# Channel attention over a 384 x 384 x 384 image: the untaken rewrite of the packed rows in two pieces instead of fourteen parts

## The chip, the cores and the metric

The kernel runs on one core of one Trainium2 chip. The metric is device time in microseconds (us). A kernel is timed in several runs, and one more execution is taken with the hardware profiler: it gives the profile page and the trace. All times inside that execution count from the start of its span, which goes from the first to the last instruction of the program.

The engines are PE (matrix multiplies), DVE (vector), ACT (scalar), POOL, and SP, which here does nothing but issue loads and wait. A name with a q (SPq, ACTq) means the engine's sequencer: transfers that it issues, branches, and instructions that only wait for or change a semaphore.

## The reference

`x` has 147,456 pixels of 384 channels in bf16. Over all pixels, each channel's mean and maximum go through a small two-layer network; the sum of both results goes through a sigmoid; and every pixel is multiplied by the 384 scales:

```python
xf = x.reshape(B, H * W, C)
gap = jnp.mean(xf, 1)
gmp = jnp.amax(xf, 1)
h_a = gap @ w1          # then the part below zero is set to zero
h_m = gmp @ w1          # likewise
scale = _sigmoid(h_a @ w2 + h_m @ w2)
return x * scale[:, None, None, :]
```

So `x` has to be read once for the scales, and then all of it has to be multiplied and written: 113 MB out, and 113 MB in at the first reading.

## The kernel before

**Rows.** The kernel lays the image out as 1,152 rows for each of the 128 partitions; a row is 384 channels of bf16, so one row over all partitions is 96 KB. `rows` is one large area of on-chip memory: five held rows, and `body` with 280 rows.

**First phase.** All rows are loaded on SP's queue (L373). PE adds them up for the mean, DVE takes the maximum into `acc` (L342). Rows that find no room are read again later. To keep more of them on the chip, 224 rows (`packed_block`, seven groups of 32) are packed: a group is four parts of eight rows, and after packing it takes up three (`homes`): two of them take the low bytes of the other two in place of their own high bytes, and the third holds the high bytes of all four in a shorter form (`pack`, L318). This shorter form holds only if the values lie in a certain range. ACT tests that on the way (`test`, L308), `judge` (L336) sums the findings, and L555 turns the sum into a flag.

**Second phase.** Once the scales are known (L433), a hand-written order takes turns: DVE multiplies a block (`multiply`, L436), ACT issues its store (`store`, L491, L492), and SP issues the next load of rows that were not kept (`read`, L518, L531) as soon as the place is free. Between them the packed groups are unpacked (`unpack`, L464), multiplied and stored (`finish`, L497). The last stores are those at L583, of ten rows kept in PSUM and of the late rows, which leave from `acc`.

**What follows the last store.** The flag is read into a register on SP, ACT and DVE (L556). `tc.If(bad != 0)` at L584 holds a rewrite: if the test failed, the packed rows are read once more, multiplied and stored over what was written. Each engine that takes part has a compare-and-branch there. If the flag is zero, it jumps over the rewrite.

**Semaphores, as the tile layer gives them out.** Each transfer adds 16 to one of eight semaphores (DMAHW0 to DMAHW7), taken in turn; DVE's instructions count up another. Whoever needs a transfer waits for its semaphore's count. Code behind the `If` has to find the same counts whichever way was taken. So the layer writes a second branch for the case "test passed": for each semaphore that the rewrite would raise, one instruction that waits until the main part's count is reached and then adds what the rewrite would have added. For the transfers' semaphores, SP has these; for DVE's count, DVE has one. The profile shows them under L584. Behind that stands the end of the program (L616, where the kernel's context is closed): SP waits for the final count of every semaphore, in seven instructions with two semaphores each, and then all engines meet at a barrier.

The instructions stand in the order of the code on each engine (`manual_schedule`, L199).

Of the kernel before, what the change touches and what calls it, by code (L numbers as in the profile page):

```python
# [9 lines left out]
ALU = mybir.AluOpType  # L10
# [22 lines left out]
PACKED = 7  # L33
# [6 lines left out]
FIRST_AT = (0, 104, 40, 64, 200, 176, 152)  # L40
FOURTH_AT = (24, 96, 32, 88, 128, 136, 144)
# [39 lines left out]
FIRST_PLACE = ((0, 8, (8, 8)), (0, 0, (8,)))  # L81
SECOND_PLACE = ((1, 0, (8, 9)), (2, 0, (10,)))
OTHER_PLACES = ((1, 17, (14,)), (2, 10, (24,)))
TEST_SCALE = 0.031187
SUM_TAIL = 4
MM_ROWS = 4
# [3 lines left out]
def kernel(  # L90
# [7 lines left out]
    nc = tc.nc  # L98
    P = nc.NUM_PARTITIONS
    B_, H, W_, C = x.shape  # L100
# [4 lines left out]
    GP = 4 * G  # L105
# [3 lines left out]
    xr = x.rearrange("b h w c -> (b h w) c")  # L109
    orr = out.rearrange("b h w c -> (b h w) c")  # L110

    def rows_of(ap, block):
        first, n = block
        return ap[first * P:(first + n) * P, :].rearrange("(p n) c -> p n c", n=n)
# [7 lines left out]
    def take(n):  # L122
        nonlocal at
        at += n
        return at - n, n
# [3 lines left out]
    packed_block = take(GP * PACKED)  # L129
# [26 lines left out]
    scale_bc = consts.tile([P, C], BF16)  # L156
# [9 lines left out]
    rows = nc.alloc_sbuf_tensor_at("rows", [P, HELD_ROWS + BODY_ROWS, C], BF16, offset=RING_BYTES).ap()  # L166
    held, body = rows[:, 0:HELD_ROWS, :], rows[:, HELD_ROWS:HELD_ROWS + BODY_ROWS, :]
    slots = [body[:, lo:lo + n, :] for lo, n in SLOTS]
    spare = body[:, SPARE, :]
    homes = [body[:, lo:lo + 3 * G, :] for lo in HOME_AT]  # L170
# [36 lines left out]
    nc.vector.memset(bank_a, 0.0)  # L207
    nc.vector.memset(test_bias, 4.5 * TEST_SCALE)
    nc.vector.memset(minus4, -4.0)
# [25 lines left out]
    for i in range(PACKED):  # L235
        if i in TOGETHER:
            lo = min(HOME_AT[i], D_AT[i % 2])
# [59 lines left out]
    def test_one(rows, k):  # L297
# [3 lines left out]
        if len(rows.shape) == 3:  # L301
            out_ = out_.rearrange("p (r n) -> p r n", r=rows.shape[1])
        nc.scalar.activation(out=out_, in_=rows, func=ACT.Square, bias=test_bias, scale=TEST_SCALE)  # L303
        nc.scalar.activation(  # L304
# [57 lines left out]
    for st in steps:  # L362
# [8 lines left out]
        _, block, rows, lo, hi = st  # L371
# [10 lines left out]
        j = max(0, min(m, A - done))  # L382
# [5 lines left out]
        while j < m:  # L388
            c, e = halves[turn % len(halves)]
# [33 lines left out]
    for q0, part_ps in tp_ps:  # L423
        n = part_ps.shape[1]
# [11 lines left out]
    def multiply(dst, src):  # L436
        n = dst.shape[1]
        nc.vector.tensor_tensor(  # L438
            out=dst, in0=src, in1=scale_bc.unsqueeze(1).to_broadcast([P, n, C]), op=ALU.mult
        )  # L440
# [16 lines left out]
    homes_d = [d_places[i % 2] for i in range(4)]  # L457
# [33 lines left out]
    def store(buf, block, lo):  # L491
        nc.scalar.dma_start(out=rows_of(orr, block)[:, lo:lo + buf.shape[1], :], in_=buf)  # L492
# [25 lines left out]
    def read(last_turn, blocks_gone):  # L518

        if not again:  # L520
            return False
        k = len(PLACES) - len(again)
        lo, n = PLACES[k]
        if lo + n > RING + 3 * G * blocks_gone or max(turn_of_row[lo:lo + n]) > last_turn:
            return False
        turn_of_row[lo:lo + n] = [k] * n
        buf, b = body[:, lo:lo + n, :], again.pop(0)
        assert b[1] == n
        j = 0
        for m in FIRST_READ if k == 0 else (n,):  # L530
            nc.sync.dma_start(out=buf[:, j:j + m, :], in_=rows_of(xr, b)[:, j:j + m, :])  # L531
            j += m
        assert j == n
        order.append((b, buf))
        return True

    def put_slot(i, lo, pieces):
        put(stay[i], slots[i][:, lo:, :], pieces, lo)
# [11 lines left out]
    read(-1, 0)  # L550
    for pieces in OTHER_PLACES:
        put_slot(*pieces)
# [7 lines left out]
    j = PLACES[-1][0] + PLACES[-1][1]  # L560
    assert j + for_psum <= PLACES[-5][0] + PLACES[-5][1]
    leaving = [(body[:, j:j + for_psum, :], first_block), (acc[:, 0:LATE_ROWS, :], late_block)]
    for turn in range(turns):
        b, buf = order.pop(0)
# [17 lines left out]
    for to, block in leaving:  # L582
        store(to, block, 0)  # L583
    with tc.If(bad != 0):  # L584
        for i in range(PACKED):
            for buf, lo in ((homes[i], FIRST_AT[i]), (homes_d[i], FOURTH_AT[i])):
                n = buf.shape[1]
                nc.sync.dma_start(out=buf, in_=rows_of(xr, packed_block)[:, lo:lo + n, :])
                multiply(buf, buf)
                store(buf, packed_block, lo)  # L590
    in_order.close()

# [28 lines left out]
```

## Time and profile before

| what | value |
|---|---|
| median of 3 runs | 725.27 us (725.21 to 725.94) |
| the profiled execution | 724.86 us, its span 723.07 us |
| busy: DVE, ACT, PE | 563.9, 349.8, 183.8 us |
| read and written | 192.14 and 113.25 MB, 422 GB/s over the span |
| shares of the queues of loads and of stores | 62.4% and 36.7% of the transfer engines' span |
| last store: issue, and time to landing | 682.98 us, 38.2 us |

How to read it: the share of a queue is the time that its packets took, against 16 transfer engines over the whole span. "Time to landing" counts from the issue of a transfer to the last raise of its semaphore. In the view of one line, the three numbers are the shortest, median and longest duration in ns, then the starts of the first and the last in us. In the view of waits, the numbers are the sum in us, how many waits, and the longest. Semaphore instructions and branches count as busy for no engine, so they stand in none of the shares of busy time.

### The profile page before, as it was taken

The numbers are of one execution on the slowest core, as the hardware profiler recorded it, in microseconds if no ns is written. First come the engines' busy times: TensorE is split into PE (matmuls) and PEld (weight loads), VectorE is DVE, ScalarE is ACT, GpSimd is POOL, SyncE is SP. The second block draws the span as 40 slices with busy tenths as digits, with TensorE's granted clock in tenths as the row PEclk, the third lists the DMA queues.
The fourth block names the chain that finished last, engine by engine and source line by source line (L and its number), as shares of the span: only waits on it lengthen the run. The fifth ranks groups of instructions, "written<-read, shape, count | busy, mean of one in ns | idle before, by whom it ended". The sixth has DMA issues, their size and how long they took to land.

```text
span 723.1 us, 3872 instructions
## 1 busy us (share of the span) xinstructions
PE 183.8 (25%) x1354; PEld 73.1 (10%) x1354; DVE 563.9 (78%) x441; ACT 349.8 (48%) x251; POOL 0.7 (0%) x6
## 2 busy tenths in 40 slices
PE   5577475966777560000000000000000000001000
PEld 1222122322222140000000000000000000001000
DVE  5698999999999998797966454798888889496200
ACT  6999999997999200057230032806244451300000
POOL 0000000000000000000000000000000000000000
PEclk9888878896978555555555555555555555555555
DMA  9999999999999979999999999999999999999997
GB/s 381 431 441 436 420 435 429 432 426 433 430 427 425 424 314 385 396 433 429 432 432 429 436 426 432 424 435 433 430 435 436 430 432 430 435 435 431 441 426 341
DMA packets 21123, 305.63 MB, mean 423 GB/s; under 512 B 2704, under 2 KB 2928, under 8 KB 8176
## 3 DMA queue, kind: packets, MB, share of 16 engines
q1 hardware_dynamic: 13760, 192.14, 62.4%
q10 hardware_dynamic: 7344, 113.25, 36.7%
q8 instruction: 10, 0.16, 0.1%
q14 instruction: 9, 0.07, 0.0%
HBM read 192.14 MB, written 113.25 MB: 422 GB/s over the span
## 4 chain that ended last, share of the span: by engine, by line
DMA 63%; DVE 28%; issue 3%; SPq 0%; DVEq 0%
DMA rows<-in_x_dram 44%; DVE acc L342 19%; DMA out_dram<-rows 18%; DVE rows L438 8%; DMA acc<-in_x_dram 1%; DVE rows L470 1%; DVE acc L438 0%; SPq L373 0%; DVE acc L475 0%; DVE acc L470 0%; SPq L531 0%; DVEq L438 0%; DVEq L342 0%
## 5 line engine op out<-in xcount | busy, mean ns | idle before, releaser
L438 DVE TENSOR_TENSOR rows<-rows,scale_bc 128x9216 bf16<-128x9216 bf16 (+9 forms) x56 | 230.9, 4166 | 93.7 <-DMA rows<-in_x_dram 92.7
L342 DVE TENSOR_TENSOR acc<-acc,rows 128x2304 bf16<-128x2304 bf16 (+4 forms) x234 | 245.2, 1126 | 12.7 <-DMA rows<-in_x_dram 12.5
L489 ACT COPY rows<-rows 128x1536 uint8<-128x1536 uint8 x28 | 41.3, 1476 | 206.4 <-DVE rows L438 205.7
L276 PE MATMUL bank_a<-rows,small 128*1 128x512 bf16 (+3 forms) x888 | 94.8, 473 | 82.0 <-DMA rows<-in_x_dram 82.0
L348 PE MATMUL words_ps<-ident_bf,acc 128*128 128x128 bf16 x24 | 2.7, 313 | 378.4 <-DVE acc L576 378.4
L303 ACT ACTIVATE rows<-rows 128x3072 uint8<-128x3072 int8 (+1 forms) x35 | 81.9, 2341 | 10.5 <-DMA rows<-in_x_dram 9.8
L304 ACT ACTIVATE rows<-rows 128x3072 uint8<-128x3072 uint8 (+1 forms) x35 | 82.0, 2344 | 1.1
L489 ACT COPY rows<-acc 128x1536 uint8<-128x1536 uint8 x42 | 60.5, 1473 | 18.2 <-DVE acc L475 17.7
L276 PEld LDWEIGHTS <-small 128*1 128x1 bf16 x888 | 30.4, 95 | 142.9 <-issue 122.0
L348 PEld LDWEIGHTS <-acc 128*128 128x128 bf16 x24 | 2.5, 148 | 378.6 <-DVE acc L576 378.6
L330 ACT COPY rows<-rows 128x1536 uint8<-128x1536 uint8 x28 | 39.7, 1468 | 0.3 <-PE words_ps L324 0.3
L324 PE MATMUL words_ps<-rows,scale_bc 128*128 128x512 fp8e4 (+1 forms) x126 | 37.0, 405 | 9.0 <-ACT rows L331 9.0
L324 PE MATMUL words_ps<-rows 128*128 128x512 fp8e3 (+1 forms) x126 | 35.1, 388 | 0.0
L470 DVE TENSOR_SCALAR rows<-rows 128x1536 uint16<-128x1536 uint16 x56 | 31.3, 560 | 1.9
L324 PE MATMUL words_ps<-rows,w_sb 128*128 128x512 fp8e3 x84 | 26.4, 398 | 0.0
L489 ACT COPY acc<-rows 128x1536 uint8<-128x1536 uint8 x14 | 20.5, 1467 | 0.0
L331 ACT ACTIVATE rows<-words_ps 128x1536 uint16<-128x1536 f32 x14 | 20.1, 1438 | 0.0
L324 PEld LDWEIGHTS <-scale_bc 128*128 128x128 bf16 x126 | 12.0, 101 | 29.2 <-issue 17.7
L324 PEld LDWEIGHTS <-rows 128*128 128x128 bf16 x126 | 12.7, 101 | 16.2 <-issue 2.4
L475 DVE SCALAR_TENSOR_TENSOR rows<-rows 128x768 uint32<-128x768 uint32 x14 | 13.4, 959 | 0.5
L475 DVE SCALAR_TENSOR_TENSOR acc<-acc,rows 128x768 uint32<-128x768 uint32 x14 | 13.4, 958 | 0.5
L286 ACT COPY w_sb<-bank_a 65x128 f32<-65x128 f32 x2 | 0.5, 261 | 25.0 <-PE bank_a L276 24.4
(61 smaller groups left out, 70.4 us busy)
## 6 DMA issues: line engine op xcount, KB each, us to landing
rows<-in_x_dram SPq DMA_DIRECT2D x16, 2880.0 KB, 26.8
out_dram<-rows ACTq DMA_DIRECT2D x15, 2880.0 KB, 21.4
rows<-in_x_dram SPq DMA_DIRECT2D x15, 2304.0 KB, 18.5
out_dram<-rows ACTq DMA_DIRECT2D x14, 2304.0 KB, 21.1
rows<-in_x_dram SPq DMA_DIRECT2D x4, 3072.0 KB, 32.1
rows<-in_x_dram SPq DMA_DIRECT2D x14, 768.0 KB, 14.0
out_dram<-rows ACTq DMA_DIRECT2D x2, 4608.0 KB, 45.6
rows<-in_x_dram SPq DMA_DIRECT2D x4, 2016.0 KB, 25.7
```

What stands on the lines that cost most here:

```text
L276: nc.tensor.matmul(sum_ps[q * QP:q * QP + 1, 0:g * P], lhsT=ones_bf[:, 0:1], rhs=rows[:, k:k + g, q * P:(q + 1) * P], start=(done + k == 0 ...
L303: nc.scalar.activation(out=out_, in_=rows, func=ACT.Square, bias=test_bias, scale=TEST_SCALE)
L304: nc.scalar.activation(out=out_, in_=out_, func=ACT.Square, bias=minus4, accum_out=tests[:, k:k + 1],)
L324: nc.tensor.matmul(words[:, c:c + BANK], lhsT=weights[2 * r + k], rhs=high(part(i, r), dt)[:, half * n + c:half * n + c + BANK], start=(r ...
L330: nc.scalar.copy(out=high(part(i, r), U8)[:, span], in_=low(part(i, r + 2), U8)[:, span])
L331: nc.scalar.activation(out=part(i, 2).rearrange("p n c -> p (n c)").bitcast(U16)[:, span], in_=words, func=ACT.Copy, bias=32767.5,)
L342: nc.vector.tensor_tensor(out=out_, in0=in0, in1=in1, op=ALU.max)
L348: nc.tensor.transpose(out=out_[:, r, q * P:(q + 1) * P], in_=rows[:, r, q * P:(q + 1) * P], identity=ident_bf)
L438: nc.vector.tensor_tensor(out=dst, in0=src, in1=scale_bc.unsqueeze(1).to_broadcast([P, n, C]), op=ALU.mult)
L470: nc.vector.tensor_scalar(out=u16(dst), in0=u16(src), scalar1=s1, scalar2=s2, op0=op0, op1=op1)
L475: nc.vector.scalar_tensor_tensor(out=u32(v), in0=u32(v), scalar=0x3F3F3F3F, in1=u32(m), op0=ALU.bitwise_xor, op1=ALU.bitwise_xor)
L489: nc.scalar.copy(out=dst, in_=src)
```

## The change

Only the body of the rewrite (the branch for "test failed") is edited. Before, it goes through the seven groups and, in each, through two parts, one of 24 rows and one of 8: load, multiply in place, store, fourteen times. After, the 224 rows are taken as two pieces of 112 rows. Each piece lies in `body` as two halves of 56 rows with a gap of `BAD_GAP` = 2 rows behind each, and is loaded by one transfer, multiplied by one instruction and stored by one transfer.

```diff
+BAD_GAP = 2
...
     with tc.If(bad != 0):
-        for i in range(PACKED):
-            for buf, lo in ((homes[i], FIRST_AT[i]), (homes_d[i], FOURTH_AT[i])):
-                n = buf.shape[1]
-                nc.sync.dma_start(out=buf, in_=rows_of(xr, packed_block)[:, lo:lo + n, :])
-                multiply(buf, buf)
-                store(buf, packed_block, lo)
+        n = GP * PACKED // 2
+        for j in range(2):
+            lo = j * (n + 2 * BAD_GAP)
+            parts = lambda rows: rows.rearrange("p (a r) c -> p a r c", a=2)
+            buf = parts(body[:, lo:lo + n + 2 * BAD_GAP, :])[:, :, 0:n // 2, :]
+            nc.sync.dma_start(out=buf, in_=parts(rows_of(xr, packed_block)[:, j * n:(j + 1) * n, :]))
+            scale = scale_bc.unsqueeze(1).unsqueeze(1).to_broadcast([P, 2, n // 2, C])
+            nc.vector.tensor_tensor(out=buf, in0=buf, in1=scale, op=ALU.mult)
+            nc.scalar.dma_start(out=parts(rows_of(orr, packed_block)[:, j * n:(j + 1) * n, :]), in_=buf)
```

In the new numbering the condition is at L586, the load at L592, the multiply at L594, the store at L595, and the program's end at L621.

The built programs differ in what follows from this. The branch with the rewrite has 21 instructions in place of 74 (SP 8 for 24, ACT 6 for 29, DVE 7 for 21). Its two loads and two stores are given DMAHW1 to DMAHW4. The branch for "test passed" has four semaphore instructions on SP, for DMAHW1 to DMAHW4, in place of eight, for DMAHW0 to DMAHW7 in this order; DVE's one adds 2 in place of 14. The instructions ahead of the branch, 3,768, are the same, and those of the end are the same but for the counts that they wait for.

## The prediction

> **What bounds the kernel now.** I read the page first: how full each engine and the transfers are, and the chain that ended last.
>
> ```profile
> span 723.1 us, 3872 instructions
> ...
> DMA  9999999999999979999999999999999999999997
> ...
> q14 instruction: 9, 0.07, 0.0%
> ...
> DMA 63%; DVE 28%; issue 3%; SPq 0%; DVEq 0%
> ```
>
> The transfers are at 90% or more in all slices but two, and the chain is made of them and of the multiplies that stand between a load and its store. The edited lines, L584 to L590, are not in that chain. So two questions remain: are they run at all, and does anything that they bring stand after the last transfer? The view of single lines answers the first, for L584 (the condition) and L616 (the end of the program, where the tile layer waits for everything):
>
> ```profile
> L584 SPq EVENT_SEMAPHORE  x8: 17/17/17, 721.2 to 721.8; - x8
> L584 SPq COMPARE_BRANCH  x1: 45/45/45, 645.5 to 645.5; - x1
> ...
> L584 DVEq EVENT_SEMAPHORE  x1: 21/21/21, 681.5 to 681.5; - x1
> L584 ACTq COMPARE_BRANCH  x1: 50/50/50, 684.2 to 684.2; - x1
> ```
>
> ```profile
> L616 SPq EVENT_SEMAPHORE  x9: 17/28/28, 721.8 to 723.0; - x9
> ...
> L616 ACTq DRAIN  x2: 8/8/8, 684.3 to 722.6; - x2
> ```
>
> Semaphore instructions of L584 exist only in the branch for "test passed", and for L588, the load in the other branch, the trace has no record. With these inputs the fourteen parts are not run: no load, multiply or store that the diff removes or adds costs anything by its own duration. What the reader is to see is the eight semaphore instructions from 721.2 to 721.8, in the last 2 us. Who they wait for is in the waits of SP, and when the stores land is in the transfers issued in the stretches 650 to 652, 664 to 666 and 681 to 684 us:
>
> ```profile
> SPq L584 <- SPq L584: 75.7, 1, 75.7
> ```
>
> ```profile
> out_dram<-rows ACTq DMA_DIRECT2D x1, 4608.0 KB, 43.6
> out_dram<-rows ACTq DMA_DIRECT2D x1, 2880.0 KB, 33.1
> ```
>
> ```profile
> out_dram<-rows ACTq DMA_DIRECT2D x1, 4608.0 KB, 47.6
> out_dram<-rows ACTq DMA_DIRECT2D x1, 2880.0 KB, 37.1
> ```
>
> ```profile
> out_dram<-rows ACTq DMA_DIRECT2D x1, 1920.0 KB, 35.6
> out_dram<-rows ACTq DMA_DIRECT2D x1, 960.0 KB, 37.5
> out_dram<-acc ACTq DMA_DIRECT2D x1, 768.0 KB, 38.2
> ```
>
> SP takes its branch at 645.5 us, comes to the first semaphore and stands 75.7 us, until 721.2. The last store is issued at 682.98 us (timeline of ACT) and lands 38.2 us later, at 721.2. So SP waits for that store, and all it does from there to 723.07 is on the path, in order, with no transfer beside it.
>
> **What stands in that tail.** Every transfer adds 16 to one of eight semaphores, DMAHW0 to DMAHW7, given out in turn. The branch that is not taken would raise them, so the passed branch has SP raise them by hand, one instruction for each semaphore that the rewrite uses: it waits for the count of the main part, then adds. Fourteen loads and fourteen stores use all eight. The first instruction waits for DMAHW0, which belongs to the last store (issued 682.98). The single records start, in us from the span's start, at 721.24 (DMAHW0), 721.33, 721.41, 721.50, 721.57, 721.65, 721.71 and 721.78 (DMAHW1 to 7), then the jump, and 721.85 is the first instruction of the end (L616), which waits for DMAHW1 and DMAHW0 together. From 721.85 to the span's end at 723.07 it is 1.23 us.
>
> **The change, part by part.**
>
> *The main part.* The instruction lists before the branch, 3,768 instructions on the five engines, are the same one by one: operations, shapes, waits, semaphores, buffers. Nothing is moved on SP's, ACT's or POOL's queue. Cost 0.
>
> *The rewrite itself.* Two loads, two multiplies and two stores in place of fourteen of each, all in the branch not taken: 0. What would be saved there if the test failed no row shows, and it isn't in the time.
>
> *SP's semaphores.* Two loads and two stores use DMAHW1 to DMAHW4 alone. So SP's passed branch falls from eight semaphore instructions to four, and DMAHW0 is no longer among them. The four that are left wait for stores issued at 637.6, 650.84, 651.2 and 664.5 us (the first a store of 6144 KB with 39.5 us to landing in the view of transfers, the others the rows shown): they land at 677.1, 683.9, 694.8 and 701.6. SP is through with them and with the jump at about 701.7, 19.5 us before the last store lands, and waits for DMAHW0 at the first instruction of the end instead. That is where the gain is: from the wake at 721.24 to the first instruction of the end at 721.85 is 0.61 us (eight steps of 65 to 94 ns, the jump within the last), and all of it goes. Four instructions vanish, and four and the jump move under the wait. What is late next is still the same store; the end's 1.23 us stays, its seven waits being the same in number. From below: if the four left ran after the last landing, only four steps would go, 4 x 0.076 = 0.30 us. From above: 0.61, the whole stretch; nothing before the landing is touched. I take 0.61, because the slack of 19.5 us is large against differences of landing.
>
> *The new wait.* SP now stands at L621 (as the end's line is numbered after) instead of L584. Behind it on SP are only the end's own waits; the other engines wait for SP at the final barrier, as before.
>
> *DVE, ACT, POOL, PE.* DVE's semaphore instruction adds 2 instead of 14, at 681.5, 40 us before the end. ACT's and DVE's jumps skip 6 and 7 instructions instead of 29 and 21. ACT's jump takes 0.14 us between its branch record (ends 684.20) and its next one (684.34); both lie under the last store. 0 on the path; without that cover ACT's would be worth less than 0.14.
>
> *Code.* 57 instructions fewer to load. Queue q14 moved nine code packets; the last one, at 650.6, took 0.31 us on one of 16 engines. If one packet fell away, 0.31/16 = 0.02 us of transfer time: between 0 and 0.02, taken as 0.
>
> **The sum.** The profiled execution took 724.86 us: span 723.07 and 1.79 around it. Span after: 723.07 - 0.61 = 722.46, time 724.25. It stood 0.41 under the median of 725.27, so the median becomes 725.27 - 0.61 = **724.66 us**, 0.08% less. The three runs lie 0.73 us apart (0.10%), so about 0.2%, 1.45 us, is what a measurement of this kernel can tell from no change, and the forecast is "no change" by that bound.
>
> **Rivals.**
>
> *Half the gain.* The four semaphores left still run after the last landing: 0.30 us, 724.97. Against it: the store on DMAHW4 lands 19.5 us earlier, and the stores of one queue landed here in the order of issue. For it: nothing. 3 in 100.
>
> *Slower: code that comes late.* The branch jumps, and a jump can need code that isn't loaded. One q14 packet starts at 650.6 us, 5.1 us after SP's compare at 645.5; if it was the target of that jump, code cost SP 5.4 us, under SP's wait of 75.7. If SP's jump to the end, or the end's own code, came to need a load after the last landing, that would be on the path. Place: between SP's records at 721.24 and 723.07. Price: at least 0.31 us (the packet), at most 5.4, nearest 2.7 (the smallest store from issue to landing, 288 KB); 2.7 gives 727.4. It decides "slower" from 0.61 + 1.45 = 2.06 us. Against it: before, SP passed the jump to the end in 66 ns with no gap, and after, it jumps 19.5 us ahead with a target 20 instructions nearer. 4 in 100.
> The Trainium skill, "Runtime: NRT & Kernel Launch", section "Instruction fetch mechanics", says that code is prefetched only in sequence and that a taken branch to a page that is not loaded waits for it. The trace bears it out as far as one late packet goes and shows no such wait on the path; by that rule alone the sum stays 724.66 while SP jumps early, and becomes this rival's if the page is missing late.
>
> *Another transfer rate.* The two data queues hold the transfer engines for 62.4% + 36.7% = 99% of the span, so one part in 500 of their rate is worth 1.4 us, over twice the forecast. A shorter program could leave buffers elsewhere in memory. No row shows such an effect; the nearest is the spread of one program, 0.10%. I bound it by twice that, 0.2% both ways: 723.2 or 726.1. 13 in 100: 7 faster than the bound (the 0.61 helps), 3 slower, 3 inside.
>
> *The change does nothing.* The wait could count as before if the last landing were not on DMAHW0; then the tail is the same, 725.27. SP's wake within 0.02 us of that landing speaks against it. 2 in 100.
>
> **How the numbers follow.** Forecast 78, half the gain 3, late code 4, rate 13, nothing 2. Within 0.2% (723.8 to 726.7): 78 + 3 + 2 + 3 and 1 of late code = 87. Faster: 7. Slower: 3 of late code and 3 of rate = 6. The likeliest case alone reaches from 725.21 - 0.61 = 724.6 to 725.94 - 0.30 = 725.6. The range takes in that, "nothing", and the near side of the faster rate: 724.0 to 725.8.
>
> **What would show it.** In the profile after: four L586 semaphore instructions on SP, starting near 677, 684, 695 and 702 us instead of eight from 721.2; SP's long wait, about 20 us, at L621; the last landing where it was; about 1.25 us instead of 1.85 from there to the span's end; no records of L592, L594, L595; the span about 722.5. A span change that comes before the last landing, or a code packet on q14 after 702 us, would make the prediction wrong.

## The result, and the profile after

The changed kernel takes 723.83 us (median of 15 runs, 723.28 to 724.79), the kernel before took 725.18 beside it (15 runs, 724.25 to 726.99). The ratio is 0.9982, with a 95% interval of 0.9974 to 0.9990: 1.35 us less, between 0.7 and 1.9. The forecast was 0.61 us less, with a range that begins at 724.0. The sign is right, more than half of the size is missing, and the time lies 0.17 us under the range.

First the page after, in the lines that answer to those shown of before:

```profile
span 722.0 us, 3868 instructions
...
DMA  9999999999999979999999999999999999999998
...
q14 instruction: 8, 0.07, 0.0%
```

The span is 1.03 us shorter (723.07 to 722.05). Transfers are as full as they were. The line to remember is the last: the code queue moved eight packets in place of nine.

Then the views of the condition (L586) and of the program's end (L621), and the waits of SP (sum, number, longest):

```profile
L586 SPq EVENT_SEMAPHORE  x4: 17/17/17, 676.9 to 701.3; - x4
L586 SPq COMPARE_BRANCH  x1: 50/50/50, 646.6 to 646.6; - x1
```

```profile
L621 SPq EVENT_SEMAPHORE  x9: 17/28/19482, 701.4 to 722.0; - x9
```

```profile
SPq L586 <- SPq L586: 54.7, 4, 30.2
SPq L621 <- DMA out_dram<-acc: 19.5, 1, 19.5
```

This is what the prediction described. The four semaphore instructions that are left run from 676.9 to 701.3 us, long before the last store lands. SP then stands 19.5 us at the first instruction of the end. The last store, in the transfers issued from 681 to 684 us, is still the one from `acc`:

```profile
out_dram<-acc ACTq DMA_DIRECT2D x1, 768.0 KB, 38.3
```

The records of the semaphores split the span in two at the last raise by that store:

| profiled execution | last landing | from there to the span's end | span |
|---|---|---|---|
| before | 721.22 | 1.85 | 723.07 |
| after | 720.83 | 1.22 | 722.05 |

So 0.63 us came out of the tail, and 0.39 us came before the last landing, where the instruction lists are the same. One execution can't carry that second number. But the code packet that stood at 650.6 us before is gone from the span; after, it starts at 723.02, 1 us behind the span's end. That made two theories. **Tail:** SP's semaphore instructions are the whole gain, 0.61 us, the rest is spread. **Code:** the missing packet counts too. Every transfer is dealt out over 16 transfer engines and has landed when the slowest is through (its semaphore is raised 16 times), so a packet that holds up one of them can hold up all.

### The profile page after: what moved, and what is told of

Its sections match the earlier page's. It is cut to its first block, busy times and chain, and to the rows that moved or that the text cites. A ratio compares the mean times of both kernels' runs of the same rounds, so it can differ in the third digit from the quotient of the medians.

```text
span 722.0 us, 3868 instructions
## 1 busy us (share of the span) xinstructions
PE 182.3 (25%) x1354; PEld 73.0 (10%) x1354; DVE 563.8 (78%) x441; ACT 349.8 (48%) x251; POOL 0.7 (0%) x6
## 4 chain that ended last, share of the span: by engine, by line
DMA 64%; DVE 25%; issue 2%; PE 1%; ACT 1%; SPq 0%; DVEq 0%; ACTq 0%
DMA rows<-in_x_dram 45%; DMA out_dram<-rows 19%; DVE acc L344 16%; DVE rows L440 8%; PE words_ps L326 1%; DVE rows L472 1%; ACT rows L332 0%; SPq L375 0%; DVE acc L440 0%; PE bank_a L278 0%; ACT rows L333 0%; DVE acc L477 0%; DVE acc L472 0%; SPq L533 0%; PE bank_a L434 0%
## 5 line engine op out<-in xcount | busy, mean ns | idle before, releaser
L278 PE MATMUL bank_a<-rows,small 128*1 128x512 bf16 (+3 forms) x888 | 90.6, 455 | 83.9 <-DMA rows<-in_x_dram 83.9
L326 PE MATMUL words_ps<-rows,scale_bc 128*128 128x512 fp8e4 (+1 forms) x126 | 38.5, 419 | 9.0 <-ACT rows L333 9.0
```

Of the source, the lines that this page charges most:

```text
L278: nc.tensor.matmul(sum_ps[q * QP:q * QP + 1, 0:g * P], lhsT=ones_bf[:, 0:1], rhs=rows[:, k:k + g, q * P:(q + 1) * P], start=(done + k == 0 ...
L326: nc.tensor.matmul(words[:, c:c + BANK], lhsT=weights[2 * r + k], rhs=high(part(i, r), dt)[:, half * n + c:half * n + c + BANK], start=(r ...
```

## The experiments

The ratios are against the kernel before in the same session (its medians: 725.28, 724.85 and 725.11 us). In all of them "tail" is the stretch from the last landing to the span's end in the profiled execution.

### The changed kernel once more, and its code moved back

The changed kernel unedited, as the yardstick for the three others of the session:

> The changed kernel itself, beside the three others on one chip. The tail theory (SP's semaphore instructions behind the last landing are the whole gain): 0.61 us under the kernel before, ratio 0.9992, and 1.22 us from the last landing to the span's end. The code theory (one code packet fewer before the last stores also counts): 0.9 to 1.35 us under it, ratio 0.9981 to 0.9988, because the transfer engine that no longer carries the packet of 0.31 us was among the last.

Measured: 724.32 us, ratio 0.9988 (0.9979 to 0.9997), 0.96 us under the kernel before; tail 1.22. In its profile the last landing is at 721.40, later than the 721.22 of before, so the 0.39 us of the first two profiles did not come again.

Then the same kernel with dead instructions on SP (`drain`, which here has nothing to do), in the branch that is not taken:

```diff
             nc.scalar.dma_start(out=parts(rows_of(orr, packed_block)[:, j * n:(j + 1) * n, :]), in_=buf)
+        for _ in range(16):
+            nc.sync.drain()
     in_order.close()
```

> As the changed kernel, but with 16 instructions more on SP inside the branch that is not taken, so that SP's code from the jump on lies where it lay before. Four semaphore instructions are left in the passed branch, as in the changed kernel. Tail theory: the same time as the changed kernel, 0.61 us under the kernel before, and 1.22 us from the last landing to the end. Code theory: the code packet on the instruction queue is back near 650 us, and the time is 0.3 to 0.7 us above the changed kernel's, with the same tail.

Measured: 724.61 us, ratio 0.9989 (0.9980 to 0.9998), 0.67 under the kernel before, tail 1.21. The packet is back; this is the code queue in the stretch from 640 to 700 us, where the changed kernel has no such line:

```profile
q14 instruction: 1, 0.01, 0.0%
```

The tail part is confirmed: with the packet in place, what is left is 0.67, the 0.61 of the forecast. The difference between the two, 0.29 us (-0.12 to 0.52), points to the code theory but isn't clear of zero. The profiles don't show it: the last landing is at 721.26 with the packet and at 721.40 without.

### Which semaphores, and how many

Four pieces of 56 rows, so that all eight semaphores are raised again:

```diff
-        n = GP * PACKED // 2
-        for j in range(2):
...
+        lo = 0
+        for n in (56, 56, 56, 56):
+            buf = body[:, lo:lo + n, :]
+            nc.sync.dma_start(out=buf, in_=rows_of(xr, packed_block)[:, lo:lo + n, :])
+            multiply(buf, buf)
+            store(buf, packed_block, lo)
+            lo += n
```

> The rewrite in four pieces of 56 rows: four loads and four stores use all eight semaphores, so the passed branch has eight semaphore instructions again and the first waits for the last store, while the code stays short. Tail theory: the gain is gone, 0.0 us against the kernel before (ratio 1.0000), and 1.85 us from the last landing to the end. Code theory: no code packet near 650 us, and 0.3 to 0.7 us under the kernel before in spite of the full tail.

Measured: 724.99 us, ratio 0.9996 (0.9987 to 1.0005), 0.29 under the kernel before. The eight instructions stand behind the last landing again, here in the views of the condition and of the end:

```profile
L586 SPq EVENT_SEMAPHORE  x8: 17/17/17, 721.1 to 721.6; - x8
```

```profile
L619 SPq EVENT_SEMAPHORE  x9: 17/28/28, 721.7 to 723.3; - x9
```

But the tail is 2.28 us, longer than the 1.85 that both theories expected. The single records show where: at the end, SP's first five instructions start 0.07 to 0.09 us apart, and the sixth 0.41 us after the fifth.

Three pieces, by the same edit with (80, 72, 72), raise six semaphores, without the last store's:

> The rewrite in three pieces of 80, 72 and 72 rows: six semaphore instructions in the passed branch, the last store's semaphore not among them. Tail theory: what counts is whether the last store's semaphore is among them, not how many there are: 1.22 us from the last landing to the end and 0.61 us under the kernel before, as with four. If each semaphore instruction counted by itself, two of eight gone: 0.15 us under it. Code theory: as the changed kernel if there is no code packet near 650 us, else 0.3 to 0.7 us above it.

Measured: 724.54 us, ratio 0.9989 (0.9980 to 0.9998), 0.74 under the kernel before. The six instructions run from 677.8 to 717.5, so it is the last store's semaphore that counts and not their number. Yet the tail is 1.67, not 1.22:

```profile
L619 SPq EVENT_SEMAPHORE  x9: 17/28/4086, 717.6 to 723.3; - x9
L619 SPq DRAIN  x3: 7/7/115, 722.1 to 722.9; - x3
```

Here the gap is between the first and the second drain: 0.38 us where the changed kernel has 0.06, and the second drain takes 115 ns in place of 7. Counted from SP's first instruction in the program's list, both late instructions are number 210. In the changed kernel SP has 209, and the last of them is the last of the end. I read this as a boundary in SP's code behind number 209. Crossing it costs SP some 0.4 us: the tails are 0.43 and 0.45 us longer than the 1.85 and 1.22 without it. A code packet follows about 1 us after the stall's beginning (723.1 us in both traces). Number 210 runs 0.6 us before that packet starts, so its code was there already. The kernel before jumped to number 209 at 645.5 and had its packet at 650.6, under its wait of 75.7 us.

These kernels also bear on the code theory. With the tail of its profile taken off each median, the runs taken beside one another here leave 723.43 and 723.40 us for the kernel before and the padded one, which have the packet, and 723.10, 722.71 and 722.87 for two, four and three pieces, which have none before the last landing: 0.3 to 0.7 us less.

### The code alone, with the old tail

The kernel before, with the rewrite's loads issued by ACT. SP keeps its eight semaphore instructions and loses 23 others, none of which is ever run:

```diff
-                nc.sync.dma_start(out=buf, in_=rows_of(xr, packed_block)[:, lo:lo + n, :])
+                nc.scalar.dma_start(out=buf, in_=rows_of(xr, packed_block)[:, lo:lo + n, :])
```

> The kernel before, with the fourteen loads of the rewrite issued by ACT instead of SP. The passed branch keeps its eight semaphore instructions on SP, but SP's code from the jump on moves 23 places forward, inside the code that is loaded. Tail theory: 1.85 us from the last landing to the end, and 0.0 us against the kernel before. Code theory: the same tail, no code packet near 650 us, the last landing 0.3 to 0.7 us earlier, and so 0.3 to 0.7 us under the kernel before.

And with SP's code padded back, by 24 drains in the same branch:

> As the run before it, with 24 instructions more on SP in the branch that is not taken, so that SP's code lies where it lay before. Both theories: eight semaphore instructions, tail 1.85 us, the code packet back near 650 us, 0.0 us against the kernel before. It tells whether ACT's longer code alone does anything.

Measured: 724.76 us without the packet (ratio 0.9997, 0.9988 to 1.0006) and 725.17 with it (1.0005, 0.9996 to 1.0014). Tails are 1.84 and 1.85. From the pages, the code queue of the one and then of the other:

```profile
q14 instruction: 8, 0.07, 0.0%
```

```profile
q14 instruction: 9, 0.07, 0.0%
```

Against the kernel before neither is clear of no change. The code theory had 0.3 to 0.7 us between the first of them and the kernel before; measured are 0.09. Against each other, with nothing different but dead code on SP, they are 0.41 us apart (0.09 to 0.83, from drawing the runs of both anew, as for the pair above), and this time the interval leaves out zero. But the padded one lies 0.32 us above the kernel before, with the same packet and the same tail, so spread or ACT's longer code may have a part in the 0.41. These runs put one packet at 0.1 to 0.4 us and no closer. With the tails taken off, these runs and those of the two kernels further down, taken beside them, leave 723.00 and 723.32 with the packet and 722.92, 722.79 and 723.21 without: here the two groups overlap.

### More packets

If one packet costs little, several should show it. The changed kernel got empty instructions that are run, where SP has only to wait:

```diff
+    for _ in range(384):
+        nc.sync.drain()
     with tc.If(bad != 0):
```

> The changed kernel with 384 empty instructions on SP between its last load and the branch, where it has 75 us to wait: three more code packets on the instruction queue between 645 and 690 us, and SP's code at the end lies in its page as in the changed kernel. Tail theory: no difference from the changed kernel, 0.6 to 1.0 us under the kernel before, tail 1.22 us. Code theory, all packets on one of the 16 transfer engines: three times 0.31, so 0.9 us above the changed kernel, about level with the kernel before, and the slowest transfer engine 0.9 us further behind the others at the last landing. Packets spread over all engines: 0.06 us.

> The same with 640 empty instructions, five more code packets. Tail theory: no difference from the changed kernel. Code theory, one engine: 1.55 us above the changed kernel, some 0.6 above the kernel before. Spread: 0.1 us above the changed kernel.

 (640 in place of 384)

Measured: 726.57 us with three packets (ratio 1.0018, 1.0009 to 1.0027), 728.36 with five (1.0040, 1.0026 to 1.0054; five runs). Both have a tail of 1.22 and wait 19.5 and 19.6 us at the end's first instruction, so SP's own time isn't it. This is the stretch from 715 us to the end, after, then with three packets, then with five; the first line is the busy share of the 16 transfer engines in forty slices, the second their rate:

```profile
DMA  9889967999979999799998999886520000000000
GB/s 527 351 351 439 395 263 307 527 439 395 483 307 483 483 395 465 325 439 413 430 456 351 386 492 456 351 351 281 211 105 35 0 0 0 0 0 0 0 0 0
```

```profile
DMA  9966999999798999999641100000000000000000
GB/s 439 470 282 251 502 439 408 439 439 439 313 489 364 502 408 401 458 408 382 282 182 50 56 31 31 25 25 25 25 25 25 25 25 0 0 0 0 0 0 0
```

```profile
DMA  5958999998999899761000000000100000000000
GB/s 219 494 247 357 466 411 466 411 466 373 444 384 428 373 450 439 329 274 44 27 27 27 27 27 27 27 27 22 44 22 22 22 22 22 0 0 0 0 0 0
```

The reader is to see the long foot, mostly at 22 to 31 GB/s. One engine's share of some 430 GB/s is 27: a single engine works on while fifteen are done. The sixteen raises of the last store's semaphore give its delay:

| kernel | code packets from 640 to 700 us | slowest engine's landing | behind the second slowest | time against before |
|---|---|---|---|---|
| changed kernel (first profile) | 0 | 720.83 | 0.04 | -1.35 |
| changed kernel (second profile) | 0 | 721.40 | 0.23 | -0.96 |
| three packets | 3 | 723.57 | 2.47 | +1.46 |
| five packets | 5 | 724.95 | 4.22 | +3.25 |

A lag alone needs no packet: in the ten kernels here that have one code packet or none from 640 to 700 us and don't run the rewrite, the slowest engine is 0.04 to 1.11 us behind the next, 1.11 in three pieces. But 2.47 and 4.22 lie far outside that.

From the -0.96 of the changed kernel's second session, three packets cost 2.42 us, 0.81 each, and five cost 4.21, 0.84 each. The landing of the slowest engine says 0.91 and 0.82 against the first profile of the changed kernel, 0.72 and 0.71 against the second. The code theory had 0.31 for each, the packet's duration, and is wrong in that; that they all fall on one engine is shown.

The single records of packets tell where most of the rest is. On one engine each packet starts some 3 ns before the one ahead of it ends, so the one that follows a code packet can be found. It takes longer than others of its size: 1.27 us in place of 0.855 (23,040 bytes) or 0.988 in place of 0.573 (15,360 bytes), and once 1.16 (23,040 bytes). With its own 0.31 to 0.33 us, a code packet holds its engine up by 0.73 us, once by 0.62. That makes 2.2 us for three and 3.6 for five; what else there is in the 2.42 and 4.21 stays open. It goes with the packet and not with the empty instructions that were run: behind the packet of the kernel before at 650.6, and in both kernels padded with dead code, the next one also takes 1.27.

One packet alone costs the kernel something between nothing and these 0.73 us, by how far its engine is from the slowest. In the profile of the kernel before, that engine can be followed from packet to packet to the end: its last packet ends at 720.59 us and the slowest engine's at 720.89, so in that execution the packet cost nothing. The 0.29 and 0.41 of the pairs are differences of medians over eleven executions each.

### Two whole pieces, and no rewrite at all

The changed kernel without halves and gap (the edit of the four pieces, with (112, 112)):

> The changed kernel without the two halves and the gap: two pieces of 112 rows, each in one stretch. The counts of instructions on each engine are the same as in the changed kernel. Both theories: the same as the changed kernel, tail 1.22 us, no code packet before the end; 0.61 us under the kernel before by the tail theory, 0.9 to 1.35 by the code theory. A difference from the changed kernel would be one of the halves.

Measured: 724.43 us, ratio 0.9995 (0.9984 to 1.0007), tail 1.22, no packet before the end. The runs lie from 723.49 to 726.94 and the interval holds both theories; it settles nothing beyond the halves bringing no gain that this could see.

Without the condition and the rewrite:

```diff
-    bad = nc.values_load(flag, engines=(ENG.SP, ENG.Activation, ENG.DVE))
...
-    with tc.If(bad != 0):
...
```

> The test's condition and the whole rewrite are left out: the kernel would not repair packed rows that failed the test. No branch, no passed branch, SP's code shorter still. Tail theory: 1.2 us from the last landing to the end, 0.6 to 0.7 us under the kernel before. Code theory: like the changed kernel, 0.9 to 1.35 us under it. If it is clearly below the changed kernel, the branches themselves cost something that neither theory has.

Measured: 723.78 us, ratio 0.9984 (0.9975 to 0.9993), 1.07 under the kernel before, tail 0.99 us. It is the fastest of its session, but it repairs nothing. The changed kernel was not in that session, so 0.11 us between it (0.96 less than before) and this one (1.07 less) is as near as the numbers come: a cost of the branch that is left can't be seen, within some tenths of a us. The tail's 0.99 has one reason in the list: the end waits for the last store in its third instruction of six instead of its first of seven, so three steps fewer stand behind the landing, 0.19 of the 0.23 us.

### What the rewrite costs when it runs

Both kernels with the flag always set (`scalar1=-0.5` in place of 0.5 at the comparison):

> The kernel before with the threshold of the flag set so that the rewrite always runs, as if the test had failed. It shows what the branch would cost: 22 MB are read and 22 MB written once more, by the rate of the page (422 GB/s) at least 104 us, so 830 us or more, and records of the lines in the rewrite. If the time stayed at 725, the rewrite would not be what the flag decides.

> The changed kernel with the rewrite always run: the same 44 MB in two loads and two stores. Load, multiply and store of a piece of 11 MB follow one another and only two pieces can overlap, so it is at least as long as the fourteen parts: 104 us of transfers, plus a multiply of 112 rows (23 us by the rate of L438, 6.16 us for 30 rows) that nothing hides: 850 us or more.

Measured, one run each: 828.58 us in fourteen parts (a little under the expected 830 or more), 827.02 us in two pieces. So the flag does decide on the rewrite, and it was not run before. The expectation for two pieces was wrong. From its views, the multiplies and the transfers issued from 700 us:

```profile
L594 DVE TENSOR_TENSOR rows<-rows,scale_bc x2: 22558/22559/22560, 747.6 to 772.9; 128x43008 bf16<-128x43008 bf16 x2
```

```profile
rows<-in_x_dram SPq DMA_DIRECT2D x2, 10752.0 KB, 40.7
out_dram<-rows ACTq DMA_DIRECT2D x2, 10752.0 KB, 28.6
```

Both loads are issued at once. The first multiply, 22.6 us, lies under the second load, the second under the first store. Two pieces are enough to keep the transfers busy.

## Why the prediction was right or wrong

**The branch is not taken, and the main part is the same.** Right: no record of the rewrite's lines after, and some 103 us more where it is forced.

**SP's semaphores.** Right in mechanism and size. The tail went from 1.85 to 1.22 us, 0.63 against the forecast 0.61; the four that are left start at 676.9 to 701.3 where 677 to 702 was forecast; the wait at the end is 19.5 us where about 20 was. With the code packet put back, the time falls by 0.67. Three pieces show that it hangs on the last store's semaphore.

**Code.** Wrong: this is the step that failed. It read "If one packet fell away, 0.31/16 = 0.02 us of transfer time: between 0 and 0.02", and with it fell the upper bound of the step on SP, "nothing before the landing is touched". It shared the packet among sixteen engines as if the work went to whichever was free. Shown is the contrary: the packets of SP's code fall on one engine, a transfer lands with its slowest engine, and each packet holds its engine up by 0.73 us by the records, 0.8 by the times of the kernels with three and five. The upper bound of the step should have been that, and neither 0.02 nor its 0.31: the nearest row gave a packet's duration and not what it does to a queue that never runs empty. What the one packet that fell away was worth is less well known: 0.29 and 0.41 us in the two pairs, 0.09 against the kernel before, nothing in the one execution in which its engine can be followed.

**The sum, mended.** 0.63 for the tail and 0.1 to 0.4 for the packet make 0.7 to 1.0 us. The 0.96 of the second session lies in that, and so does the lower end of the first one's interval (0.7 to 1.9). What else there is in the 1.35 isn't told apart from spread: the same kernel took 723.83 us in the first session and 724.32 in the second, which is inside the range. A step was wrong; that the first time fell 0.17 us under the range is luck in part.

**Half the gain, and "does nothing".** Fell, as forecast: the last landing is DMAHW0's, and all four came early.

**Code that comes late.** It did not happen in this kernel, but the place and the condition are real. The changed kernel has 209 instructions on SP; three pieces have 213, four pieces 216, and these two pay 0.4 us in the tail. The forecast price of 2.7 us was far too high. By the reading above, the changed kernel escapes it closely: its end has its last instruction just ahead of the boundary.

The Trainium skill, "Runtime: NRT & Kernel Launch", section "Instruction fetch mechanics", calls the cost of crossing into the next block of code mostly hidden. Here it is not: 0.4 us on SP's path where it falls in the tail, and up to 0.8 us for a packet under full queues.

**The signs of being wrong.** Both came: a code packet after 702 us, but at 723.02, behind the span and at no cost to it; and 0.39 us of the span ahead of the last landing. The trace of before doesn't put that 0.39 down to the packet, since the packet's engine was not the slowest there.

**Another transfer rate.** The bound of 0.2% happened to hold the effect, but the mechanism named, buffers elsewhere in memory, was not tested. The transfers' mean rate didn't change (423 GB/s both).

**The range.** Its lower edge took the near side of that rival only. With 0.73 us as the code step's upper end, for one packet on the slowest engine, it would have begun at 725.27 - 0.61 - 0.73 = 723.9 before any spread.

## What to carry to other kernels

Code that is never run still counts twice: by the semaphores that the passed branch has to raise by hand, above all the last transfer's, and by where it puts the code behind it. When all transfer queues are full, price a stray packet by what it does to one engine, up to the slowest engine's place, and not by its share of sixteen. Let an engine with a long wait before the end cross into its last code under that wait and not behind it.

## What was not expected of the hardware

A code packet of 8 KB, 0.31 us by its record, delays a saturated transfer engine by 0.73 us: the packet of data behind it takes 1.27 us in place of 0.855. Other engines don't take over its work: with five such packets it finishes 4.22 us behind the next. Crossing the boundary in its code costs SP 0.43 to 0.45 us by the tails, and the packet that goes with it starts only 0.6 to 0.7 us after the late instruction, so the stall isn't a wait for that packet. Which of the 16 engines carries SP's code, and why the packet of data behind a code packet takes longer, stays open.
